# Query and key projections cut into two halves of 64 tokens, each on one half of TensorE's columns

## The chip, the cores and the metric

The kernel runs on one core of one Trainium2 chip. The metric is the time of one execution on the device, in microseconds (us); lower is better.

## What is computed

Linear attention over 4 batches, 4 heads, 1088 tokens and 32 dimensions per head, then two feed-forward layers on the 4352 x 128 result. The part that matters here is the feature map: queries and keys are multiplied by two small matrices, and the outer product of the two results is the feature vector.

```python
def phi(x):
    a = np.einsum('rd,bhsd->bhsr', S1, x)      # r = 8, d = 32
    b = np.einsum('rd,bhsd->bhsr', S2, x)
    return np.einsum('bhsi,bhsj->bhsij', a, b).reshape(*x.shape[:-1], r * r)
q_p, k_p = (phi(q), phi(k))
kv = np.einsum('bhsf,bhsd->bhfd', k_p, v)
z = np.sum(k_p, axis=2)
num = np.einsum('bhsf,bhfd->bhsd', q_p, kv)
den = np.einsum('bhsf,bhf->bhs', q_p, z)[..., None] + 1e-06
```

Behind it follow a gated feed-forward layer (rms norm, `silu(x @ w_gate) * (x @ w_val) @ w_out`, 1536 hidden) and a mixture layer with 32 slots. All of them are float32.

## The kernel before

The tokens are worked in nine tiles T of 512 (the last has 256). For every tile the feed-forward layer runs over f, twelve blocks of 128 hidden units: `ff_in` (mm3 at L635 to L637, called three matmuls a product, because each operand is split into a high and a low part), `ff_gate` (silu on ACT, product on DVE), `ff_high` and `ff_low` (the split of the hidden block) and `ff_out`. These 128x512 matmuls fill most of TensorE's time. In the first tile, `ff_out` takes whole float32 operands instead (L690).

Between them, attention for the next tile is worked in small steps. `k_chain(b)` prepares the keys of a batch: DVE transposes 32x32 blocks (L338), `Keys.project(g)` multiplies by `bdf`, a 128x64 matrix with S1 and S2 of four heads on its diagonal blocks, `halves` copies one half of the result (L279, ACT), `outer` forms the feature vectors (L284, DVE), and `sum` (L386) multiplies them with the values; the two heads of a pair go to partitions from 0 and from 64. `q_chain(T)` does the same for queries: `shuffle` (L495), `project` (L500), `halves`, `outer`, `back`, `attend` (L523; L530 for the last tile), division, rms norm, and a transposition (L584). `r_chain(T)` takes the layer's result to the mixture layer (L707, L710, L717).

In `project`, the tokens are the stationary operand (the weight load, 128 columns for 128 tokens) and `bdf` is the moving one (64 columns). Each projection writes 128 tokens x 64 values into a PSUM bank. A batch of keys has two groups (g = 0 and 1) of four such projections and a third group of 64 tokens left over (g = 2, through the transposition L341 of a 64-row tile); a tile of queries has four, the last tile two. A projection is one instruction of the program and, in float32, two passes in the trace, each a weight load (PEld) and a matmul (PE).

The first tile's attention and the first weights' conversion to float32 (`conv_w`, `f64_words`) are the front: its order is a table, `FRONT`, with filler matmuls (`keep_busy`, L298) between the steps, in which `kp:0`, `kp:1`, `qp` and `kp:2` are the projections. The front ends near 23.5 us. After it, a planner orders the instructions of each engine by its own model of their durations, within what data and the written order of some steps (`in_order`) allow. So a step's instructions can lie apart or between those of another step, and an edit to one step can move others.

Of the kernel before, what the change touches and what calls it, by code (L numbers as in the profile page):

```python
# [16 lines left out]
P = 128  # L17
# [31 lines left out]
def body(ctx, tc, q, k, v, s1, s2, wg, wv, wo, rg, phi, w1, w2, out):  # L49
    nc = tc.nc  # L50
    pe, act, dve, pool = nc.tensor, nc.scalar, nc.vector, nc.gpsimd
# [217 lines left out]
    bdf = bd.rearrange("p h r -> p (h r)")  # L269
# [39 lines left out]
    def bank():  # L309
        if not free:  # L310
            return aux()
        free.append(free.pop(0))
        tag = free[-1]
        return ps.tile([P, 512], F32, tag=tag, name=tag, bufs=3 if tag == "aux" else 2)

    class Keys:
# [34 lines left out]
        def project(self, g):  # L351
            n, pp = self.size(g)
            self.a[g] = bank()
            for t in range(n):
                o = self.a[g][:pp, 64 * t : 64 * t + 64]
                pe.matmul(o, self.kT[g][:, P * t : P * t + pp], bdf, start=True, stop=True)  # L356

        def halves(self, g, both=False):
            n, pp = self.size(g)
# [122 lines left out]
    class Queries:  # L482
# [14 lines left out]
        def project(self):  # L497
            self.a["q"] = bank()
            for h in range(self.n):
                pe.matmul(self.a["q"][:, 64 * h : 64 * h + 64], self.qD[:, P * h : P * h + P], bdf, start=True, stop=True)  # L500

        def halves(self):
            self.pq = work()[:, 0 : 256 * self.n].rearrange("p (f g n) -> p f g n", f=2, n=D)
# [664 lines left out]
    for T in range(NTILE):  # L1168
# [10 lines left out]
        o = [ps.tile([P, 512], F32, tag="gv"[(T + e) % 2], name="fo", bufs=2) for e in range(2 if T == 0 else 1)]  # L1179
# [54 lines left out]
```

## Time and profile before

| | us |
|---|---|
| median of 3 runs | 322.39 (322.32 to 322.49) |
| profiled execution | 322.96 |
| its span | 321.2 |
| PE busy | 308.1 |
| DVE busy | 235.7 |
| ACT busy | 185.8 |
| POOL busy | 61.8 |

The span runs from the first to the last instruction of the profiled execution; its own time holds some 1.8 us more around it. PE is TensorE's matmuls and PEld its weight loads, which overlap with PE. Matmuls are pipelined, so one row's duration is longer than the distance to the next row's start; how long a step takes is read from the starts.

### The profile page before, as it was taken

What the parts mean: (1) busy time and instruction counts of PE and PEld (TensorE: products, weight loads), DVE (VectorE), ACT (ScalarE), POOL (GpSimd) and SP (SyncE); (2) the same over time, 40 slices, a digit from 0 to 9 for tenths busy, and PEclk for the clock granted to TensorE, in tenths of its full rate; (3) what the DMA queues carried; (4) which work ended last, traced back from release to release, by engine and by line L of the source; (5) the groups of instructions that cost most, each with busy time, mean ns of one, the idle gap of its engine ahead of it and who ended that gap; (6) DMA issues with size and microseconds to landing.
All of it is one profiled execution on the core that took longest, in us unless ns stands there. A gap on an engine that the chain in (4) does not pass through costs nothing.

```text
span 321.2 us, 5509 instructions
## 1 busy us (share of the span) xinstructions
PE 308.1 (96%) x2011; PEld 244.7 (76%) x2011; DVE 235.7 (73%) x457; ACT 185.8 (58%) x417; POOL 61.8 (19%) x104
## 2 busy tenths in 40 slices
PE   8979989999999999999999999999999999999992
PEld 5756645788887878888888788888887878898482
DVE  4779966695888776966988858668778666664762
ACT  3767374456646457566563666565565665566451
POOL 3346499800021120001010100010020100003120
PEclk9999999999999999999999999999999999999998
DMA  7988000000007000000080000000890493000017
GB/s 200 300 292 207 5 0 1 2 0 2 0 3 204 1 2 0 2 0 0 4 202 1 3 0 2 0 0 14 299 230 2 138 300 87 0 2 0 2 40 241
DMA packets 31131, 22.40 MB, mean 70 GB/s; under 512 B 13056, under 2 KB 27136, under 8 KB 31104
## 3 DMA queue, kind: packets, MB, share of 16 engines
q1 hardware_dynamic: 30928, 21.98, 23.7%
q8 instruction: 16, 0.26, 0.4%
q10 hardware_dynamic: 176, 0.07, 0.2%
q14 instruction: 11, 0.09, 0.1%
HBM read 19.81 MB, written 2.23 MB: 69 GB/s over the span
## 4 chain that ended last, share of the span: by engine, by line
PE 82%; POOL 4%; DVE 4%; DMA 3%; SPq 2%; ACT 1%; issue 1%; DVEq 0%; POOLq 0%
PE v L635 7%; PE g L636 7%; PE g L635 7%; PE v L636 7%; PE v L637 7%; PE g L637 7%; PE o L637 7%; PE o L635 7%; PE o L636 6%; PE aux L523 3%; PE aux L386 2%; SPq L77 2%; DMA g_sb<-in_moe_rms_g_dram 2%; PE aux L356 2%; PE o L690 2%; PE aux L500 2%
## 5 line engine op out<-in xcount | busy, mean ns | idle before, releaser
L665 ACT ACTIVATE silu<-g 128x512 f32<-128x512 f32 (+1 forms) x103 | 60.3, 592 | 36.1 <-PE g L637 32.9
L675 ACT CAST hh<-hf 128x512 fp32r<-128x512 f32 x89 | 54.9, 617 | 39.3 <-DVE hf L666 37.9
L666 DVE TENSOR_TENSOR hf<-v,silu 128x512 f32<-128x512 f32 (+1 forms) x91 | 61.3, 679 | 20.3 <-PE v L637 12.4
L680 DVE TENSOR_TENSOR hl<-hf,hh 128x512 fp32r<-128x512 f32 x89 | 60.8, 687 | 17.6 <-ACT hh L675 15.9
L635 PE MATMUL g<-xh,wgh 128*128 128x512 f32 (+1 forms) x108 | 42.7, 398 | 2.1 <-ACT xh L591 0.9
L635 PE MATMUL v<-xh,wgh 128*128 128x512 f32 (+1 forms) x108 | 42.7, 396 | 0.6 <-DVE hh L666 0.6
L636 PE MATMUL g<-xh,wgl 128*128 128x512 f32 (+1 forms) x108 | 41.5, 384 | 0.8 <-POOL wgl L245 0.8
L636 PE MATMUL v<-xh,wgl 128*128 128x512 f32 (+1 forms) x108 | 42.0, 389 | 0.0
L637 PE MATMUL v<-xl,wgh 128*128 128x512 f32 (+1 forms) x108 | 41.0, 380 | 0.0
L637 PE MATMUL g<-xl,wgh 128*128 128x512 f32 (+1 forms) x108 | 41.0, 379 | 0.0
L635 PE MATMUL o<-hh,woh 128*128 128x512 f32 (+1 forms) x94 | 36.8, 392 | 0.0
L637 PE MATMUL o<-hl,woh 128*128 128x512 f32 (+1 forms) x94 | 36.6, 389 | 0.0
L636 PE MATMUL o<-hh,wol 128*128 128x512 f32 (+1 forms) x94 | 35.6, 379 | 0.0
L571 POOL TENSOR_SCALAR rs<-ss 128x4 f32<-128x4 f32 (+1 forms) x8 | 2.9, 356 | 130.2 <-ACT sq L564 130.2
L635 PEld LDWEIGHTS g<-xh,wgh 128*128 128x128 f32 x108 | 20.2, 188 | 9.5 <-ACT wgh L238 2.4
L636 PEld LDWEIGHTS g<-xh,wgl 128*128 128x128 f32 x108 | 20.4, 188 | 5.2 <-POOL wgl L245 1.7
L635 PEld LDWEIGHTS v<-xh,wgh 128*128 128x128 f32 x108 | 20.3, 188 | 5.2 <-DVE hh L666 1.0
L637 PEld LDWEIGHTS v<-xl,wgh 128*128 128x128 f32 x108 | 20.3, 188 | 4.3 <-issue 0.5
L636 PEld LDWEIGHTS v<-xh,wgl 128*128 128x128 f32 x108 | 20.4, 188 | 4.1 <-issue 0.5
L637 PEld LDWEIGHTS g<-xl,wgh 128*128 128x128 f32 x108 | 20.3, 188 | 3.7
L284 DVE TENSOR_TENSOR work<-asb,aux 128x512 f32<-128x512 f32 (+2 forms) x25 | 19.4, 804 | 2.4 <-ACT asb L279 2.3
L637 PEld LDWEIGHTS o<-hl,woh 128*128 128x128 f32 x94 | 17.7, 188 | 3.2 <-issue 0.2
(255 smaller groups left out, 515.1 us busy)
## 6 DMA issues: line engine op xcount, KB each, us to landing
ring<-in_moe_w_dram SPq DMA_DIRECT2D x12, 256.0 KB, 7.4
ring<-in_moe_w_dram SPq DMA_DIRECT2D x5, 512.0 KB, 5.8
ring<-in_k_dram SPq DMA_DIRECT2D x8, 256.0 KB, 3.1
qt<-in_q_dram SPq DMA_DIRECT2D x4, 512.0 KB, 5.4
ring<-in_v_dram SPq DMA_DIRECT2D x16, 128.0 KB, 4.6
ring<-in_moe_w_gate_dram SPq DMA_DIRECT2D x6, 256.0 KB, 8.2
ring<-in_moe_w_val_dram SPq DMA_DIRECT2D x6, 256.0 KB, 6.8
ring<-in_moe_w_out_dram SPq DMA_DIRECT2D x3, 512.0 KB, 4.9
```

The lines of the kernel that those rows point to most:

```text
L77: i = (on or nc.sync).dma_start(out=out, in_=in_)
L284: on.tensor_tensor(out=dst.rearrange("p g (r s) -> p g r s", s=R), in0=x1.unsqueeze(3).to_broadcast([pp, n, r, R]), in1=x2.unsqueeze(2).to ...
L356: pe.matmul(o, self.kT[g][:, P * t : P * t + pp], bdf, start=True, stop=True)
L386: pe.matmul(self.a["kv", hp][64 * h2 : 64 * h2 + D1, 64 * hp : 64 * hp + 64], va[:, h, 2 * i + g, :] if t < 8 else vr[:, h, :], self.pk[hp ...
L523: pe.matmul(o, pD[:, f, h, :], rhs, start=(f == 0), stop=(f == 1))
L635: first = pe.matmul(o, ah, bh, start=start, stop=False)
L636: pe.matmul(o, al, bh, start=False, stop=False)
L637: last = pe.matmul(o, ah, bl, start=False, stop=stop)
L665: mark["silu"] = act.activation(s[:, cs], g[:, cs], AF.Silu).ins
L666: mark["gate"] = mark["gate", T, f] = dve.tensor_tensor(out=hf32[T, f][:, cs], in0=v[:, cs], in1=s[:, cs], op=ALU.mult).ins
L675: act.copy(hh[T, f], hf32[T, f])
L680: dve.tensor_tensor(out=hl[T, f], in0=hf32.pop((T, f)), in1=hh[T, f].bitcast(F32), op=ALU.subtract)
```

## The change

Each projection of 128 tokens becomes two of 64 tokens. The first writes partitions 0 to 63 of the bank, the second partitions 64 to 127, so the two use different halves of TensorE's columns. The moving operand stays `bdf`, 64 columns, so each half streams as many columns as the whole did; its weight load has 64 columns instead of 128. The projections of 64 left-over tokens stay as they are. All 128 rows of the array are used, as before. 66 projections become 132; nothing else is edited.

```diff
--- before.py
+++ after.py
@@ -352,8 +352,10 @@
             n, pp = self.size(g)
             self.a[g] = bank()
             for t in range(n):
-                o = self.a[g][:pp, 64 * t : 64 * t + 64]
-                pe.matmul(o, self.kT[g][:, P * t : P * t + pp], bdf, start=True, stop=True)
+
+                for p in range(0, pp, 64):
+                    o = self.a[g][p : p + 64, 64 * t : 64 * t + 64]
+                    pe.matmul(o, self.kT[g][:, P * t + p : P * t + p + 64], bdf, start=True, stop=True)
 
         def halves(self, g, both=False):
             n, pp = self.size(g)
@@ -497,7 +499,9 @@
         def project(self):
             self.a["q"] = bank()
             for h in range(self.n):
-                pe.matmul(self.a["q"][:, 64 * h : 64 * h + 64], self.qD[:, P * h : P * h + P], bdf, start=True, stop=True)
+                for p in range(0, P, 64):
+                    o = self.a["q"][p : p + 64, 64 * h : 64 * h + 64]
+                    pe.matmul(o, self.qD[:, P * h + p : P * h + p + 64], bdf, start=True, stop=True)
 
         def halves(self):
             self.pq = work()[:, 0 : 256 * self.n].rearrange("p (f g n) -> p f g n", f=2, n=D)
```

Where lines of the change are named, `Keys.project` is at L358 and `Queries.project` at L504; lines behind are moved by 2 or 4 (mm3 is at L639 to L641, the sums of L386 at L388).

The planner's order moves with it. Three places, all on PE:

The queries of tile 3, behind the transposition L584 of tile 2's attention (T is the transposed queries, bd the matrix of S1 and S2, aux a PSUM bank). Before:

```order
L635 MATMUL o<-hh,woh 128x512
L636 MATMUL o<-hh,wol 128x512
L637 MATMUL o<-hl,woh 128x512
L584 MATMUL aux<-ident,x 128x128 x4
L500 MATMUL aux<-bd,T 128x64 x4
L635 MATMUL o<-hh,woh 128x512
L636 MATMUL o<-hh,wol 128x512
L637 MATMUL o<-hl,woh 128x512
L635 MATMUL o<-hh,woh 128x512
```

And with the change:

```order
L639 MATMUL o<-hh,woh 128x512
L640 MATMUL o<-hh,wol 128x512
L588 MATMUL aux<-ident,x 128x128 x4
L504 MATMUL aux<-bd,T 64x64 x5
L641 MATMUL o<-hl,woh 128x512
L504 MATMUL aux<-bd,T 64x64 x3
L639 MATMUL o<-hh,woh 128x512
L640 MATMUL o<-hh,wol 128x512
L641 MATMUL o<-hl,woh 128x512
```

Four projections in one run became eight halves in two runs, of five and three, with one feed-forward matmul between them.

The queries of tile 4. Before:

```order
L635 MATMUL o<-hh,woh 128x512
L636 MATMUL o<-hh,wol 128x512
L500 MATMUL aux<-bd,T 128x64
L637 MATMUL o<-hl,woh 128x512
L500 MATMUL aux<-bd,T 128x64 x3
L635 MATMUL o<-hh,woh 128x512
L636 MATMUL o<-hh,wol 128x512
L637 MATMUL o<-hl,woh 128x512
```

With the change:

```order
L639 MATMUL o<-hh,woh 128x512
L640 MATMUL o<-hh,wol 128x512
L504 MATMUL aux<-bd,T 64x64
L641 MATMUL o<-hl,woh 128x512
L504 MATMUL aux<-bd,T 64x64 x4
L639 MATMUL o<-hh,woh 128x512
L640 MATMUL o<-hh,wol 128x512
L504 MATMUL aux<-bd,T 64x64 x3
L641 MATMUL o<-hl,woh 128x512
L639 MATMUL g<-xh,wgh 128x512
```

Runs of one and three projections became runs of one, four and three halves.

The left-over keys of the last batch, ahead of the key sums (work holds the feature vectors, va the values). Before:

```order
L636 MATMUL g<-xh,wgl 128x512
L637 MATMUL g<-xl,wgh 128x512
L356 MATMUL aux<-bd,T 64x64
L635 MATMUL v<-xh,wgh 128x512
L636 MATMUL v<-xh,wgl 128x512
L637 MATMUL v<-xl,wgh 128x512
L386 MATMUL aux<-work,va 33x64 x16
L635 MATMUL o<-hh,woh 128x512
```

With the change:

```order
L640 MATMUL g<-xh,wgl 128x512
L641 MATMUL g<-xl,wgh 128x512
L358 MATMUL aux<-bd,T 64x64
L388 MATMUL aux<-work,va 33x64 x16
L639 MATMUL v<-xh,wgh 128x512
L640 MATMUL v<-xh,wgl 128x512
L641 MATMUL v<-xl,wgh 128x512
```

The 64-token projection, which stood alone between feed-forward matmuls, now stands directly ahead of the sums.

## Rows read from the trace of the kernel before

**Rows 1.** Stretches: busy us (instructions) of PE, PEld, DVE, ACT, POOL; clock, DMA, GB/s.
```profile
28.00:56.00 28.00, 25.36 (x101) 15.62 (x99) 22.56 (x40) 15.18 (x33) 22.09 (x31) 1.00 0.16 37
56.00:292.00 236.00, 235.71 (x1452) 194.59 (x1451) 178.52 (x326) 140.44 (x304) 22.00 (x41) 1.00 0.19 51
```

**Rows 2.** Timeline of PE, a run of four: start us, us, instructions.
```profile
67.96 0.39 PE L635 MATMUL o<-hh,woh 128*128 128x512 f32 x1
68.19 0.39 PE L636 MATMUL o<-hh,wol 128*128 128x512 f32 x1
68.42 1.00 PE L500 MATMUL aux<-bd,T 128*128 128x64 f32 x8
...
69.54 0.39 PE L635 MATMUL g<-xh,wgh 128*128 128x512 f32 x1
```

**Rows 3.** Timeline of PE, a run of two projections.
```profile
164.02 0.39 PE L637 MATMUL v<-xl,wgh 128*128 128x512 f32 x1
164.24 0.55 PE L356 MATMUL aux<-bd,T 128*128 128x64 f32 x4
...
164.92 0.39 PE L636 MATMUL g<-xh,wgl 128*128 128x512 f32 x1
```

**Rows 4.** Timeline of PE, a 64-token projection and the key sums.
```profile
115.66 0.39 PE L637 MATMUL g<-xl,wgh 128*128 128x512 f32 x1
115.97 0.33 PE L356 MATMUL aux<-bd,T 128*64 128x64 f32 x2
116.23 0.50 PE L635 MATMUL v<-xh,wgh 128*128 128x512 f32 x1
116.57 0.39 PE L636 MATMUL v<-xh,wgl 128*128 128x512 f32 x1
116.80 0.40 PE L637 MATMUL v<-xl,wgh 128*128 128x512 f32 x1
117.13 1.09 PE L386 MATMUL aux<-work,va 128*33 128x64 f32 x32
...
118.48 0.40 PE L636 MATMUL o<-hh,wol 128*128 128x512 f32 x1
```

**Rows 5.** Timeline of PE around L530; then what runs between 246.1 and 246.2 us.
```profile
245.86 0.39 PE L637 MATMUL o<-hl,woh 128*128 128x512 f32 x1
246.18 1.17 PE L530 MATMUL aux<-kvr,work 128*64 128x132 f32 x16
...
247.62 0.40 PE L636 MATMUL v<-xh,wgl 128*128 128x512 f32 x1
...
246.18 0.34 PE L530 MATMUL aux<-kvr,work 128*64 128x132 f32 x2
```

**Rows 6.** Weight loads of L356: timeline; then count, ns min/median/max, shapes.
```profile
9.55 0.19 PEld L356 LDWEIGHTS g<-bd,T 128*64 128x64 f32 x2
...
L356 PEld LDWEIGHTS g<-bd,T x10: 133/192/192, 7.3 to 9.6; 128*128 128x128 f32 x8, 128*64 128x64 f32 x2
```

**Rows 7.** Timeline of PE around the transposition L341.
```profile
56.18 0.27 PE L341 MATMUL aux<-ident,kr 64*128 64x64 f32 x1
56.38 0.66 PE L356 MATMUL aux<-bd,T 128*128 128x64 f32 x4
```

**Rows 8.** Timeline of PE around a run of two and a 64-token projection.
```profile
62.81 0.59 PE L690 MATMUL o<-hh,ring 128*128 128x512 f32 x1
63.23 0.81 PE L356 MATMUL aux<-bd,T 128*128 128x64 f32 x6
...
64.31 0.40 PE L636 MATMUL g<-xh,wgl 128*128 128x512 f32 x1
```

**Rows 9.** Timeline of ACT in the front, with its wait.
```profile
18.10 0.67 ACT L188 ACTIVATE cvt<-ring 128x512 f32<-128x512 f32 x1 [1.96 <-DMA ring<-in_moe_w_val_dram]
...
19.23 0.29 ACT L564 ACTIVATE sq<-x 128x128 f32<-128x128 f32 x1
```

**Rows 10.** Timeline of PE, its one wait between 56 and 292 us.
```profile
97.60 0.50 PE L635 MATMUL g<-xh,wgh 128*128 128x512 f32 x1 [0.27 <-ACT silu L665]
```

## The prediction

> **What bounds the kernel now.** I read the page first: of the engines PE is busy longest, 308.1 of 321.2 us. Then the stretches [rows 1]: from 56 to 292 us, at the full granted clock (1.00), PE is busy 235.71 of 236.00 us, while DVE and ACT have 57 and 96 us to spare. There every added 0.1 us of PE time is 0.1 us of the result. From 28 to 56 PE idles 2.6 us, waiting for the conversion of weights; before 28 us it runs filler matmuls. So I price the change on PE, stretch by stretch, from rows of single runs of matmuls. PE works in steps: a 128x512 feed-forward matmul starts every 0.23 us [rows 2], the yardstick below.
>
> **What a projection costs now.** The trace shows each projection as two passes (x8 for four), each with its own weight load. The run of four begins at 68.42; from the step before it (68.19) to the second step after it (69.54) are 1.35 us, less two steps of 0.23 is 0.89, or 0.223 us a projection [rows 2]. The run of two, 164.02 to 164.92, gives 0.44, again 0.22 [rows 3]. A run thus has no fixed price: the loads follow each other 0.11 us apart under the streams, and the neighbours are of the same full shape.
>
> **What a half projection will cost.** Runs on half the columns exist already. The 64-token projection of keys (128x64 weights, 64 streamed columns: exactly the new instruction) stands alone at 115.97. From 115.66 to 116.57 are 0.91 us, less 0.46: 0.45 us for only two passes [rows 4]. The sums of L386, which alternate between the two column halves with 33-wide weights and 64 streamed columns, take 1.68 - 0.46 = 1.22 us (116.80 to 118.48) for 32 passes [rows 4]. Counting two passes on opposite halves as one round, 0.45 = F + 2r and 1.22 = F + 16r: a round costs r = 0.055 us, and entering and leaving the half shape costs a fixed F = 0.34 us a run. The rows show where F lies: 0.31 us instead of 0.23 before the run (115.66 to 115.97), a first load that nothing hides, and a step of 0.34 after it (116.23 to 116.57).
>
> The round of the new shape, 64-wide weights with 64 streamed columns on both halves, isn't in the trace. Below it is the sums' 0.055. Above it is L530: 64-wide weights and 132 streamed columns on both halves, 245.86 to 247.62, so 1.30 us for 8 rounds; less F that is 0.12 a round [rows 5]. Its two halves do start together: two matmuls run in the first 0.02 us [rows 5]. I take 0.057, by the sums, because the stream is the same as theirs and two 64-wide loads are not further apart than that even on one half (0.19 us for two of at least 133 ns, so at most 0.057, [rows 6]). For F the same rows give 0.32 (sums, with rounds of 0.056) to 0.40 (L530, with rounds of 0.113); I take 0.35, one hundredth over the solved value for the second half that starts behind the first.
>
> So a run of n projections cost 0.223n and will cost 0.35 + 0.057 x 2n: 0.58 against 0.45 for two, 0.81 against 0.89 for four, 1.26 against 1.78 for eight. **Three projections is the break-even**, and the order of the program decides which lengths there are.
>
> **The sum after the front.** In the order of before, 54 projections stand in 21 runs there, most of two or four. 54 x 0.223 = 12.0 us go. In the new order the planner cuts the halves into 25 runs, some of odd length: 8, 4, 4, 5, 4, 8, 5, 3, 4, 4, 8, 1, 4, 3, 3, 3, 2, 4, 4, 8, 4, 4, 5, 3, 4 halves. An odd run pays a full round for its last half, so the rounds sum to 118 instead of 108.
> - rounds: 118 x 0.057 = 6.7 us
> - fixed price: 25 x 0.35 = 8.8 us
> - two pairs of runs lie around the 64-row transposition L341, which already breaks the sequence (0.20 us from it to the next run, [rows 7]). At the first, one F falls away but a second unhidden load stays: -0.30. At the second, attention (L523) stands on the other side, so only one run touches it, and I take a third of that: -0.10
> - of the three 64-token projections after the front, one stood behind a run of two and cost 1.50 - 0.42 - 0.23 - 0.45 = 0.40 us more (62.81 to 64.31, with 0.42 for the step of L690, [rows 8]); it now lies in the run of five and is in the rounds: -0.40. Another moves directly ahead of the L386 sums and shares their F: 0.45 - 0.11 = -0.34. The third stays alone: 0.
>
> 6.7 + 8.8 - 0.4 - 0.74 - 12.0 = +2.4 us. The run of eight near 28.6 us, which would be 0.08 cheaper, lies where PE waits anyway, which leaves 2.4 as it is to the digit given.
>
> **The front.** There the runs are long (sixteen halves of keys, eight of queries with the 64 left-over keys), and the halves do save PE time: a projection takes two rounds, 0.11 us, instead of 0.22, so twelve save up to 1.3 us, and the key sums could start that much sooner. I cost this at nothing. The cover is the load of the first weights: ACT waits 1.96 us for it until 18.10, and the squares of the first query tile stand behind that conversion in ACT's order, at 19.23 [rows 9]. The change moves neither ACT's nor DVE's order in the front, nor any DMA. If the cover were gone, up to 1.3 us would come off.
>
> **Other engines.** POOL's and SP's orders stay the same. ACT and DVE get the same instructions, in places in another order. Each halves copy (L279) waits for the last pass of its projections, which comes some 0.2 us sooner in a run of four and about when it did in a run of two; from 56 us on PE waits for another engine only once, for ACT (0.27 us, [rows 10]), and added PE time widens that slack.
>
> **Result.** The profiled execution took 322.96 us (span 321.2), 0.57 over the median of the runs. Its own time would become 325.4; against the median of 322.39 I forecast **324.8 us**. With F from 0.32 to 0.40 the sum goes from +1.6 to +3.6.
>
> **Rivals.**
> - *Shape changes cost less than in the rows.* If 25 runs paid no F, the streams alone would count: 6.7 instead of 12.0, about 317 us. The sign turns where F falls below 0.35 - 2.4/25 = 0.25 us. For it: the rounds do overlap two halves. Against it: three kinds of runs on column halves give 0.32, 0.34 and 0.40. The Trainium skill, "TensorEngine Tiling (Array Packing)", section Theoretical Speedup, promises up to 2x where the small dimension is at most 64; by that alone the 12.0 us would halve, to about 316 us. The trace bears this out for the rounds, 0.055 for two passes instead of 0.11 each, but not for a run of two or four with its F. Chance 0.07.
> - *Loads don't hide under streams.* Then a round costs a 64-wide load and a stream one after the other, 0.057 [rows 6] and 0.055 [rows 4], 0.11 us, and 118 rounds add 118 x 0.053 = 6.3 us: about 331 us. The Trainium skill, "TensorE: Matmul & The Clock Gate", Part 3, says that a weight load overlaps running matmuls only where the row groups differ; both halves here use all rows, so by that rule this would come. The trace disagrees: the sums use all rows too (128*33 in [rows 4]) and their rounds take 0.055. Chance 0.08.
> - *The front counts after all*: 1.3 us off, 323.5 us. Against it: the wait for the load. Chance 0.09.
> - *The pieces that could give way give way together.* The old order's wait at 97.60 (0.27 us, [rows 10]) falls away in the new one, F is 0.32 (0.75 less) and the front gives its 1.3: 2.4 - 2.3 = +0.1, so about 322.5 and no difference. New waits can come in the new order just as well. Chance 0.08.
>
> **How the numbers follow.** The forecast has 0.68. About 0.2% (0.64 us) is what a measurement can tell from no change. Faster: the first rival, 0.07. Same: the last, 0.08. Slower: the forecast, the loads and the front, 0.85. The range leaves out the first two rivals and keeps the others: 322.5 (the last rival's time) to 327.2 (the 326.0 of F = 0.40 and rounds of up to 0.067).
>
> **What would show it.** In the profile after: a run of eight halves spans about 0.5 us from first to last pass, the step into a run from a 512-column matmul is 0.31 to 0.32 us, the first step behind it 0.34; the projections' groups shrink in busy time while the feed-forward groups' mean durations grow a little; PE stays full from 56 to 292 us and that stretch grows by 2 to 3 us; the squares near 19.2 us don't move. I am wrong if a run of four halves costs under 0.4 us (fixed price too high), if eight halves span 0.9 us (loads not hidden), or if the change of time lies outside 56 to 292 us.

## The result: 3.4 us slower

The changed kernel takes 325.72 us (median of 4 runs, 325.33 to 326.15), the kernel before beside it 322.36 (321.97 to 322.49): 1.0103 times as long, 95% interval 1.0086 to 1.012. Timed again with the last experiments it took 325.29 against 322.39, 1.0096 (1.0074 to 1.0118). So the loss is 2.9 to 3.4 us, where +2.4 was forecast: right in sign, inside the range, and 0.5 to 1.0 us too small.

The profiled execution took 326.15 us, its span is 324.3. The engines' busy times on its page (us, share of the span, instructions):

```profile
PE 310.6 (96%) x2143; PEld 240.4 (74%) x2143; DVE 235.5 (73%) x457; ACT 186.2 (57%) x417; POOL 60.3 (19%) x104
```

PE is 2.5 us busier than before (308.1), with 132 matmuls more, though its weight loads fell from 244.7 to 240.4 us. DVE, ACT and POOL have not moved by more than 1.5 us. PE was the bound and became a longer one. The stretch that answers to [rows 1] shows it full, as the prediction had it:

```profile
56.00:292.00 236.00, 235.35 (x1523) 187.91 (x1520) 176.60 (x320) 137.57 (x299) 19.96 (x39) 1.00 0.19 51
```

The rows that answer to those of before, from PE's timeline (start us, us, what, count). First a run of eight halves, a tile of queries, where [rows 2] had four whole projections:

```profile
67.52 0.39 PE L640 MATMUL o<-hh,wol 128*128 128x512 f32 x1
67.84 0.69 PE L504 MATMUL aux<-bd,T 128*64 128x64 f32 x16
68.45 0.50 PE L641 MATMUL o<-hl,woh 128*128 128x512 f32 x1
68.79 0.39 PE L639 MATMUL g<-xh,wgh 128*128 128x512 f32 x1
```

The step into the run is 0.32 us, the one behind its first neighbour 0.34, where 0.23 is usual; all sixteen passes lie within the 0.61 us from 67.84 to 68.45. Together 68.79 - 67.52 - 0.46 = 0.81 us, against 0.89 whole. Then four halves of keys, where [rows 3] had a run of two:

```profile
165.49 0.39 PE L641 MATMUL v<-xl,wgh 128*128 128x512 f32 x1
165.80 0.45 PE L358 MATMUL aux<-bd,T 128*64 128x64 f32 x8
166.19 0.50 PE L639 MATMUL g<-xh,wgh 128*128 128x512 f32 x1
166.52 0.39 PE L640 MATMUL g<-xh,wgl 128*128 128x512 f32 x1
```

That is 1.03 - 0.46 = 0.57 us against 0.44. From 0.57 = F + 4r and 0.81 = F + 8r follow r = 0.06 and F = 0.33; the prediction had 0.057 and 0.35. And here is another tile of queries, which the planner cut into one, four and three halves:

```profile
127.22 0.39 PE L640 MATMUL o<-hh,wol 128*128 128x512 f32 x1
127.53 0.33 PE L504 MATMUL aux<-bd,T 128*64 128x64 f32 x2
127.79 0.50 PE L641 MATMUL o<-hl,woh 128*128 128x512 f32 x1
128.22 0.45 PE L504 MATMUL aux<-bd,T 128*64 128x64 f32 x8
128.61 0.50 PE L639 MATMUL o<-hh,woh 128*128 128x512 f32 x1
128.94 0.40 PE L640 MATMUL o<-hh,wol 128*128 128x512 f32 x1
129.27 0.45 PE L504 MATMUL aux<-bd,T 128*64 128x64 f32 x6
129.65 0.50 PE L641 MATMUL o<-hl,woh 128*128 128x512 f32 x1
129.98 0.39 PE L639 MATMUL g<-xh,wgh 128*128 128x512 f32 x1
```

Five feed-forward steps of 0.23 lie in these 2.76 us, which leaves 1.61 for the sixteen passes: twice the 0.81 of the same work in one run. What the prediction did not have is L534, the last tile's attention, which is no part of the edit. [Rows 5] had its sixteen passes in one run of 1.30 us; now they are twelve and four:

```profile
250.43 0.39 PE L641 MATMUL v<-xl,wgh 128*128 128x512 f32 x1
250.75 1.11 PE L534 MATMUL aux<-kvr,work 128*64 128x132 f32 x12
...
252.13 0.40 PE L639 MATMUL o<-hh,woh 128*128 128x512 f32 x1
...
255.10 0.39 PE L641 MATMUL g<-xl,wgh 128*128 128x512 f32 x1
255.42 0.67 PE L534 MATMUL aux<-kvr,work 128*64 128x132 f32 x4
...
256.35 0.40 PE L640 MATMUL v<-xh,wgl 128*128 128x512 f32 x1
```

1.70 - 0.46 = 1.24 and 1.25 - 0.46 = 0.79, 2.03 us in all: 0.73 us more. Only a part of this is a second fixed price. In the trace of the change the four passes at 255.42 start 0.11 to 0.16 us apart and so do the last four of the twelve: the cut left eight passes with no partner on the other column half. In the one run of before a pass starts every 0.056 us on average from the second round on. Eight times 0.056 is 0.45 us, an estimate from these starts; the other 0.28 is near F.

### The profile page after: what moved, and what is told of

Its sections match the earlier page's. It is cut to its first block, busy times and chain, and to the rows that moved or that the text cites. A ratio compares the mean times of both kernels' runs of the same rounds, so it can differ in the third digit from the quotient of the medians.

```text
span 324.3 us, 5777 instructions
## 1 busy us (share of the span) xinstructions
PE 310.6 (96%) x2143; PEld 240.4 (74%) x2143; DVE 235.5 (73%) x457; ACT 186.2 (57%) x417; POOL 60.3 (19%) x104
## 4 chain that ended last, share of the span: by engine, by line
PE 82%; DMA 5%; DVE 4%; SPq 3%; POOL 2%; issue 1%; ACT 1%; DVEq 0%; POOLq 0%
PE g L639 7%; PE v L639 7%; PE g L640 7%; PE v L640 7%; PE g L641 7%; PE v L641 7%; PE o L641 7%; PE o L639 6%; PE o L640 6%; DMA ring<-in_moe_w_gate_dram 4%; PE aux L527 4%; SPq L77 3%; PE aux L388 2%; PE o L694 2%; PE aux L504 2%; DMA kr<-in_k_dram 2%
## 5 line engine op out<-in xcount | busy, mean ns | idle before, releaser
L639 PE MATMUL g<-xh,wgh 128*128 128x512 f32 (+1 forms) x108 | 43.3, 403 | 2.7 <-ACT wgh L238 1.2
L639 PE MATMUL v<-xh,wgh 128*128 128x512 f32 (+1 forms) x108 | 43.2, 400 | 0.0
L641 PE MATMUL g<-xl,wgh 128*128 128x512 f32 (+1 forms) x108 | 41.5, 384 | 0.0
L641 PE MATMUL v<-xl,wgh 128*128 128x512 f32 (+1 forms) x108 | 41.3, 382 | 0.0
L641 PE MATMUL o<-hl,woh 128*128 128x512 f32 (+1 forms) x94 | 36.9, 393 | 0.0
L639 PE MATMUL o<-hh,woh 128*128 128x512 f32 (+1 forms) x94 | 36.8, 392 | 0.0
L639 PEld LDWEIGHTS g<-xh,wgh 128*128 128x128 f32 x108 | 20.4, 189 | 9.8 <-ACT wgh L238 2.5
L639 PEld LDWEIGHTS v<-xh,wgh 128*128 128x128 f32 x108 | 20.6, 191 | 4.5 <-issue 0.7
L641 PEld LDWEIGHTS v<-xl,wgh 128*128 128x128 f32 x108 | 20.5, 189 | 4.2 <-issue 0.2
L641 PEld LDWEIGHTS g<-xl,wgh 128*128 128x128 f32 x108 | 20.5, 189 | 4.1 <-issue 0.2
L641 PEld LDWEIGHTS o<-hl,woh 128*128 128x128 f32 x94 | 17.6, 188 | 3.9 <-issue 0.4
```

What stands on the lines that cost most here:

```text
L639: first = pe.matmul(o, ah, bh, start=start, stop=False)
L641: last = pe.matmul(o, ah, bl, start=False, stop=stop)
```

## The measure used below

Times of single runs scatter by 0.5 us or more, and the kernel before was timed anew beside each set of experiments (322.57, 322.12 and 322.39 us), so times of different sets are compared by their ratios to it. The experiments are also compared on one stretch of their profiles: from the start of the first feed-forward matmul to that of the last group (L690 of the kernel before). For the kernel before, profiled once more, and the change, profiled once more (timelines of PE; the second number is the row's length):

```profile
22.40 0.50 PE L635 MATMUL g<-xh,wgh 128*128 128x512 f32 x1 [0.93 <-ACT xh L591]
...
290.95 1.03 PE L690 MATMUL o<-hf,work 128*128 128x256 f32 x4
```

```profile
22.30 0.50 PE L639 MATMUL g<-xh,wgh 128*128 128x512 f32 x1 [0.93 <-ACT xh L595]
...
294.12 1.03 PE L694 MATMUL o<-hf,work 128*128 128x256 f32 x4
```

268.55 and 271.82 us, so +3.27. The first profile of before has 268.41 there: the stretch repeats to 0.14 us, though the two executions differ by 1.16 us ahead of it. The table has every run; "fixed" is what F = 0.35 a run and 0.057 a round give for that kernel's own list of runs; a cut of L534 is in it with the measured 0.73.

| kernel | stretch, us over before | fixed | time, us | ratio to before (95%) |
|---|---|---|---|---|
| the change, first profile | +3.73 | +3.1 | 325.72 | 1.0103 (1.0086 to 1.012) |
| change_again | +3.27 | +3.1 | 325.29 | 1.0096 (1.0074 to 1.0118) |
| front_only | +0.08 | 0.0 | 321.56 | 0.9965 (0.9951 to 0.9979) |
| mid_only | +3.24 | +3.1 | 325.20 | 1.0085 (1.0067 to 1.0102) |
| whole_together | -0.58 | 0.0 | 321.84 | 0.9972 (0.996 to 0.9985) |
| halves_together | -1.38 | -0.6 | 321.28 | 0.9957 (0.9943 to 0.9972) |
| before_again | 0 | 0 | 321.8 | one run |
| l534_whole | +2.65 | +2.35 | 324.72 | 1.0078 (1.0059 to 1.0098) |
| keys_only | +0.36 | +0.2 | 321.63 | 0.9983 (0.9971 to 0.9995) |
| queries_only | +2.99 | +3.2 | 324.11 | 1.006 (1.004 to 1.0079) |
| before_longer | 0.00 | 0.0 | 321.57 | 0.9973 (0.9962 to 0.9984) |
| halves_in_long_runs | +1.46 | -1.75 | 323.47 | 1.0035 (1.0024 to 1.0045) |
| long_runs_longer | +1.27 | -1.75 | 322.44 | 1.0008 (0.9993 to 1.0024) |

## The experiments

The theory is that each run of halves between full-width matmuls has a fixed price, so that the number of runs decides. Its rivals: halves are dearer each, wherever they stand; or the new order brings waits.

**Where the loss is: the front or behind it.** front_only takes the halves for the first batch's keys and the first tile's queries alone:

```diff
+            w = 64 if self.b == 0 else pp
...
+                for p in range(0, pp, w):
+                    o = self.a[g][p : p + w, 64 * t : 64 * t + 64]
+                    pe.matmul(o, self.kT[g][:, P * t + p : P * t + p + w], bdf, start=True, stop=True)
```

and likewise `w = 64 if self.T == 0 else P` for queries.

> Halves only in the first batch's keys and the first tile's queries; every other projection whole, and the order after the front as before. Prediction on record (front hidden by the weights' load): 322.4, no difference. Theory 'runs' as the profile after suggests (long runs save PE time; at the 60 us mark the changed kernel was 0.65 us ahead): about 321.7, ratio 0.998, and the feed-forward steps after 62 us 0.5 to 0.7 us earlier than before all the way to the end. Rival 'halves' (each half costs more wherever it stands, 0.037 us apiece): about 323.2.

mid_only has `self.b > 0` and `self.T > 0` in these places.

> Halves everywhere but in the front; order after the front as in the changed kernel. Theory 'runs': all of the loss and none of the front's gain, 322.4 + 3.4 + 0.65 = 326.4, ratio 1.0125. If the front had hidden nothing and given nothing: 325.7, as the changed kernel.

The whole loss is behind the front: mid_only has +3.24 us of the change's 3.27 in the stretch, front_only +0.08, and both begin it where before_again does (22.50, 22.40 and 22.40 us; single executions differ there, see below). Why does the front give nothing, when its projections do get shorter? DVE's timeline of before_again:

```profile
9.94 0.41 DVE L284 TENSOR_TENSOR pkr<-asb,g 64x256 f32<-64x256 f32 x1 [1.08 <-ACT asb L279]
...
11.48 0.51 DVE L193 TENSOR_SCALAR cvt<-cvt 128x512 f32<-128x512 f32 x1
```

and of front_only:

```profile
9.31 0.41 DVE L284 TENSOR_TENSOR pkr<-asb,g 64x256 f32<-64x256 f32 x1 [0.20 <-ACT asb L279]
...
11.49 0.43 DVE L193 TENSOR_SCALAR cvt<-cvt 128x512 f32<-128x512 f32 x1 [0.57 <-ACT cvt L188]
```

The feature vectors of the left-over keys, and those behind them, come 0.63 us sooner, and DVE then waits 0.57 us for the first weights' conversion, which starts the next step at the same time as before. The front's saving is real and is lost to that wait. front_only's time is 1.0 us under before all the same; some 0.7 of that lies behind the last matmul and goes without halves too, as before_longer shows below, and the other 0.3 is within the interval. mid_only has the same 0.7 in its favour, so its time shows 2.6 us of loss where its stretch shows 3.24.

**The same instructions in fewer runs.** `tc.high_priority()` around the two project loops, and around L534, makes the planner put most of them out in one piece. whole_together is the kernel before with it:

```diff
+            with tc.high_priority():
+                for t in range(n):
+                    o = self.a[g][:pp, 64 * t : 64 * t + 64]
+                    pe.matmul(o, self.kT[g][:, P * t : P * t + pp], bdf, start=True, stop=True)
```

> Whole projections as before, but those of one step get priority in the planner, which puts most of them into one run (four instead of one and three, or two and two). Theory 'runs': whole projections have no fixed price, so joining them gains nothing: 322.4 within 0.3. Rival 'order' (the new order's waits cost, not the shape): a shift of 1 us or more either way from reordering alone.

halves_together is the change with the same lines.

> The change, with the same priority: 17 runs of halves after the front instead of 25, mostly of eight, and L534 in one run again. Theory 'runs': 81 fewer... by the sum, 0.35 a run and 0.057 a round: -0.6 against before after the front and -0.65 in it, so 321.1, ratio 0.996, 4.5 us under the changed kernel. Rival 'halves': as many halves, so as slow as the changed kernel, 325.7. Rival 'order': moves as whole_together does, from 325.7.

This is the sharpest test: halves_together has as many halves as the change, 2143 matmuls, and takes 321.28 us: by the ratios some 4.5 us less, in the stretch 4.65. It is faster than before. Halves are thus not dearer each. Between the two versions kept together the halves gain 0.80 us in the stretch (formula 0.6), where with the planner's cuts they lose 3.3. A part of the better times belongs to the order: before_again has two waits of PE behind 56 us (grouped waits: us in total, times, longest), of which the first profile of before had only the first,

```profile
PE g L635 <- ACT silu L665: 0.3, 1, 0.3
PE aux L341 <- DMA kr<-in_k_dram: 0.2, 1, 0.2
```

and in both kernels kept together neither is left, which is up to 0.5 of whole_together's 0.58 us.

**The kernel before once more.** In all profiles taken since the first one of before, the stretch began 0.7 to 1.3 us earlier than there.

> The kernel before, profiled once more. In every profile taken since, the first feed-forward matmul starts some 1.0 us earlier than in the first profile of before (22.5 us from the span's start, against 23.56 there), also where the front of the program was left as it was. If that is a matter of the one execution, this profile shows it near 22.5 us and no wait of ACT near 2 us for the second value weights; if it belongs to the program (the order in which SP hands out the transfers), it shows 23.5 us and a wait near 2 us again.

It is a matter of the execution. ACT's timeline in before_again, for [rows 9]:

```profile
15.84 0.68 ACT L188 ACTIVATE cvt<-ring 128x512 f32<-128x512 f32 x1
...
18.07 0.31 ACT L564 ACTIVATE sq<-x 128x128 f32<-128x128 f32 x1 [0.98 <-DVE x L541]
```

The value weights, for whose load ACT waited until 18.10 in [rows 9], are there at 15.84, and the squares wait for DVE instead, 1.16 us earlier than there.

**L534 alone.** The change, with the priority around L534 and nothing else:

```diff
-                for e in range(2):
+                with tc.high_priority():
+                    for e in range(2):
...
```

> The change, with the attention matmuls of the last tile (line 534 of the change) kept together as one run of 16 passes; everything else as in the change. Theory 'runs' (each run of halves between full-width matmuls has a fixed price): the run cut into 12 and 4 passes cost 2.03 us against 1.30, so this one is 0.7 us under the change, near 324.9. Theory 'halves' (each half dearer wherever it stands): no difference to the change, 325.6. Theory 'order' (waits from the new order): no difference beyond 0.3.

PE's timeline:

```profile
250.29 0.39 PE L641 MATMUL v<-xl,wgh 128*128 128x512 f32 x1
250.61 1.17 PE L534 MATMUL aux<-kvr,work 128*64 128x132 f32 x16
...
252.05 0.40 PE L639 MATMUL o<-hh,woh 128*128 128x512 f32 x1
```

1.76 - 0.46 = 1.30 us, as before. The stretch is 0.62 us shorter than change_again's, and by the ratios (1.0078 against 1.0096 and 1.0103) the time 0.6 to 0.8 us. The cut of L534 is about a fifth of the loss.

**Keys and queries apart.** keys_only leaves `Queries.project` as it was, queries_only `Keys.project`.

> Halves for the keys alone; the queries projected whole, as before. Behind the front these are 22 of the 54 projections. Theory 'runs': the keys stand in runs of four or eight halves, break-even or nearly so, +0.2 us behind the front, and with the earlier start that the other kernels show, near 321.8. Theory 'halves': 22 of 54 parts of the loss of 3.4 us behind the front, +1.4, near 323.0. Theory 'order': the reordering around the query runs is gone, so near 321.8 as well.

> Halves for the queries alone; the keys projected whole, as before. Theory 'runs': the planner cuts the queries into runs of two to five halves and the attention of the last tile into two, +3.1 us behind the front (of it 0.7 for the attention), near 324.8. Theory 'halves': 32 of 54 parts of 3.4 us, +2.0, near 323.6. Theory 'order': as 'runs', in waits ahead of the query runs instead of in the runs.

The stretches add up: +0.36 and +2.99 make 3.35, against 3.27 for both. Counted again, the keys have 24 of the 54 projections behind the front (the expectations say 22) and bring a tenth of the loss; the queries' 30 and L534, which is cut in queries_only too, bring the rest. Were halves dearer each, it would be 1.5 and 1.9. Nor is it waits: queries_only has none on PE behind 56 us, and change_again has the two of before_again, 0.3 and 0.2 us. The difference is the runs. In keys_only the keys stand in ten runs there, all of four halves or more; in queries_only the queries stand in fifteen, seven of them of three halves or fewer.

**The time behind the last matmul.** In the profiles of four kernels the span ends 4.8 us behind the last matmul, in those of before, the change, the two kept together and l534_whole 5.3 to 6.0 us.

```diff
-        for _ in range(n):
-            pe.matmul(idle[0][:, 0:256], hot[:, 0:P], hot, start=True, stop=True)
+        for _ in range(n):
+            w = 128 if len(idle) < 25 else 256
+            idle[len(idle)] = None
+            for c in range(0, 256, w):
+                pe.matmul(idle[0][:, c : c + w], hot[:, 0:P], hot[:, c : c + w], start=True, stop=True)
```

> The kernel before, with the first 24 of the idle matmuls at its start issued as two of 128 columns instead of one of 256: the same stream, but 24 more matmuls and loads in TensorE's program. In the profiles so far the time behind the last matmul comes in two sizes, 5.5 to 6.0 us (before, the change, whole_together, halves_together, l534_whole) and 4.8 us (front_only, mid_only, keys_only, queries_only); in the first five SP's third transfer of the output takes 1.5 to 2.0 us to issue instead of 0.33, and a 16 KB packet of the queue that brings TensorE's program lands just ahead of it. Theory 'fetch': that packet comes some 60 TensorE instructions ahead of the end, its place goes by the program's length modulo 256, and 48 more instructions move it out of the way: 0.7 us under the kernel before, near 321.6, with 4.8 us behind the last matmul. Rival: the two sizes have another cause (the halves in the front, the planner's order): no difference to before.

321.57 us, 0.8 under before, with the same filler stream cut into 24 matmuls more. SP's queue at the end in before_again (start us, us to issue):

```profile
311.04 0.36 SPq L1196 DMA_DIRECT2D out_dram<-hf  x1
311.59 1.51 SPq L1196 DMA_DIRECT2D out_dram<-hh  x1
313.19 0.38 SPq L1196 DMA_DIRECT2D out_dram<-hl  x1
```

and in before_longer:

```profile
311.54 0.36 SPq L1199 DMA_DIRECT2D out_dram<-hf  x1
312.10 0.33 SPq L1199 DMA_DIRECT2D out_dram<-hh  x1
312.91 0.33 SPq L1199 DMA_DIRECT2D out_dram<-hl  x1
```

One issue is held for 1.2 us, and the end comes 5.5 us behind the last matmul instead of 4.8. Some 0.7 us of the times of front_only, mid_only, keys_only and queries_only is this, more than the whole gain of keys_only (0.5). The hold goes by the program's length: it is there in all seven profiles with 2011 or 2143 matmuls, smaller (0.85 us, one issue later) with 2139, and absent with 2035 (twice), 2075, 2079, 2119 and 2163. The traces bear out what was put down ahead of the run: the packet of program moved out of the way. The view of the DMA queues counts packets by their start; q8, called instruction there, is the queue of the program. In before_again, from 310.5 to 313 us:

```profile
q8 instruction: 1, 0.02, 3.2%
```

and in before_longer from 305 to 309.9 us, with none from 310.5 to 313:

```profile
q8 instruction: 1, 0.02, 1.5%
```

In before_again this 16 KB packet runs from 311.43 to 312.72 us, within the held issue (311.59 to 313.10); in before_longer from 309.74 to 310.92, where the first output issue begins. So it is in all profiles: in the seven with the long hold such a packet is under way when the held issue starts, or starts within 0.1 us, and the issue ends 0.3 to 0.4 us after it landed; with 2139 matmuls it runs from 313.02 to 314.28, the issue at 313.10 still takes 0.33 us, and the next, from 313.92, is held until 314.77; in the six without the hold no such packet is under way during these issues. Why the packet holds an issue, and why not that one, stays open. The change has the hold as the kernel before has it, so its loss is not touched by this.

**As few and as long runs as possible.** halves_in_long_runs transposes both groups of keys first and projects them in one run of sixteen halves (in two of the three batches behind the front; the planner cut the other into four, four and eight); the last tile's two projections stay whole. The new lines stand in place of the loop over the two groups:

```diff
+        yield POST, 1
+        with tc.issue_after(mark["gate"]):
+            k.transpose(0)
+            k.transpose(1)
+        yield PE, 0
+        with tc.high_priority():
+            k.project(0)
+            k.project(1)
+        yield POST, 1
+        k.halves(0)
+        k.outer(0)
+        k.transpose(2)
+        yield POST, 0
+        k.halves(1)
+        k.outer(1)
+        k.copy(2)
+        yield PE, 0
...
+            w = 64 if self.T < 8 else P
```

> Halves in as few and as long runs as the program allows: the project loops are given to the planner in one piece (high priority), the two groups of keys are transposed first and projected in one run of 16 halves, the last tile's queries (two projections, under the break-even of three) stay whole, and the attention of the last tile stays one run. Theory 'runs': the formula with F = 0.35 us per run and 0.057 us per two halves gives 1.75 us less than before, near 320.5. Theory 'halves': as many halves as in the change, so near 325. Theory 'order': waits for the transposes that now stand ahead of both groups eat part of it, 320.5 to 322.5. Theory 'fetch': its program is as long as the change's within 8 instructions, so it keeps the 5.5 us or more behind the last matmul.

long_runs_longer is this with the filler matmuls cut as in before_longer.

> As halves_in_long_runs, with the idle matmuls at the start cut as in before_longer. Theories 'runs' and 'fetch' together: 1.75 + 0.7 us less than before, near 319.9. If 'fetch' is wrong: the same as halves_in_long_runs.

A miss: 323.47 us, some 2 over halves_together. Waits came in, some of them in the middle of the feed-forward work, as the theory 'order' feared, though for more than transposes. PE's timeline of halves_in_long_runs around a batch of keys, and later:

```profile
55.08 1.15 PE L357 MATMUL aux<-bd,T 128*64 128x64 f32 x32
...
56.74 0.33 PE L357 MATMUL aux<-bd,T 128*64 128x64 f32 x2 [0.30 <-ACT T L344]
57.48 1.09 PE L387 MATMUL aux<-work,va 128*33 128x64 f32 x32 [0.41 <-DVE work L284]
...
61.55 0.53 PE L387 MATMUL aux<-work,va 128*33 128x64 f32 x12
...
62.90 0.31 PE L387 MATMUL aux<-work,va 128*33 128x64 f32 x4
...
129.12 0.40 PE L646 MATMUL o<-hl,woh 128*128 128x512 f32 x1
129.72 0.50 PE L644 MATMUL g<-xh,wgh 128*128 128x512 f32 x1 [0.20 <-ACT xh L600]
```

The projections are as cheap as computed: 32 passes, sixteen halves, in 1.15 us. But the copies and outer products of two groups now fall on ACT and DVE in one burst. The key sums (L387) wait for it and come in five pieces instead of one, and some feed-forward steps stand up to 0.76 us apart instead of 0.23 (0.60 in the rows) because their operands are converted late. By PE's starts the five pieces cost 4.3 us, where before_again's one run of sums costs 2.4, and four late steps behind 129 us 1.4 more: together about the 3.2 us by which the stretch missed the formula. The long runs were paid for elsewhere. long_runs_longer is 1.0 us faster; in the two profiles 0.2 of it lies in the stretch and 0.4 behind the last matmul, where the hold is gone. halves_together with a program length without the hold was not tried.

**The change again.**

> The change itself, beside the others on this chip: near 325.6, 3.2 to 3.4 us over before. If the half clock at 22 to 26 us in its first profile was a matter of that execution, this profile shows full clock there and the feed-forward matmuls behind it some 0.3 us earlier; if it belongs to the change, it shows it again.

The half clock was that execution's. Stretches of the change's first profile, then of change_again (busy us of PE, PEld, DVE, ACT and POOL, granted clock, DMA share, GB/s):

```profile
22.00:26.00 4.00, 3.49 (x9) 2.71 (x10) 3.07 (x5) 3.02 (x7) 1.95 (x3) 0.58 0.34 83
```

```profile
22.00:26.00 4.00, 3.60 (x14) 2.44 (x14) 3.44 (x6) 3.68 (x8) 2.16 (x4) 1.00 0.52 163
```

Nine matmuls instead of fourteen run there; the two levels of the clock are 1.2 and 2.4 GHz. By PE's starts the first eight feed-forward steps took 3.46 us instead of 1.95, but the two stretches end with 0.46 us of difference: change_again then waits 0.7 us for DVE's gate product (hh), which the slower execution does not, and the rest is not taken apart.

## Why the prediction was right, and its sum too small

- **The bound.** Right: the loss is PE time behind the front, in both profiles of the change and in mid_only.
- **What whole projections cost, and the round r.** Right. Runs of eight and four halves took 0.81 and 0.57 us as computed (0.81 and 0.58). The two halves' streams and loads overlap: sixteen passes in 0.61 us. With this the rival "loads don't hide" falls; its rule, of the Trainium skill, "TensorE: Matmul & The Clock Gate", Part 3, is not borne out by these rows, whose halves use all rows of the array.
- **The fixed price F.** Right: 0.33 by the rows of the change. With F the formula gives -0.6 for the halves kept together and +3.2 for queries_only, where -0.8 (beside whole_together) and +2.99 were measured; were halves dearer each, it would be +3.3 and +1.9. The rival "shape changes cost less" falls. Its rule, of the Trainium skill, "TensorEngine Tiling (Array Packing)", Theoretical Speedup, says up to 2x; the longest run behind the front in these kernels, sixteen halves, comes to 0.35 + 16 x 0.057 = 1.26 by the formula against 1.78 whole, 1.4x, and a run of four halves to 0.57 against 0.44, which is a loss.
- **The sum.** The step that failed is the list of what is re-cut. It followed the 25 runs of projections, and the three 64-token ones, but not the other column-half work in the planner's order, of which L534 lost its one run and, for half of its passes, the partner on the other column half: +0.73 us by the rows, 0.62 by l534_whole. 2.4 + 0.73 = 3.1, and the stretch has 3.27. The row of L530 stood in the prediction as a bound for r, and was not looked for in the new order.
- **The front.** The value, nothing, was right, but by luck: the cover was named wrongly. It is not the load of [rows 9], which was late in that one execution only, and the squares did move (18.07 in before_again, 18.18 in the change's first profile). It is a conversion of weights on ACT, for which DVE waits.
- **Other engines.** The slack of the one wait, 0.27 us at 97.60 [rows 10], was to widen so that the wait fell away; that did not come, in both profiles of the change PE still waits 0.3 us there.
- **The size.** 3.27 us in the stretch became 2.9 to 3.4 us in the medians; the ends of the executions, 0.2 us apart, account for part of that spread.

## What to carry to other kernels

Two halves on opposite columns do run side by side, but each run of them between full-width matmuls costs a fixed 0.33 to 0.35 us here, so count runs, and passes left without a partner, not instructions: a split pays from four whole projections upwards and loses below three. Ask the scheduler's order for the lengths of the runs, of all work in that shape and not only of what was edited, and keep a run together before splitting it: the priority alone turned a loss of 1% into a gain of 0.4%. Longer runs are not free either, since they hand their readers a burst.

## What the runs showed of the hardware that was not expected

- The issue of one output transfer was held by 1.0 to 1.7 us beyond its usual 0.33 in seven profiles, each time with a 16 KB packet of the program queue under way; in before_longer, with 24 matmuls more in the program, the packet came 1.7 us earlier and no issue was held. Some 0.7 us of the time hang on it. A kernel with a few instructions more can be faster for no reason of its own work.
- The same load of the same program was waited for until 18.10 us in one execution and was there by 15.84 in another; the first feed-forward matmuls stand 1.16 us apart.
- The same program had a granted clock of 0.58 from 22 to 26 us in one execution and 1.00 in another. PE had sat idle 0.93 us in both just ahead of the first feed-forward matmul. It came once more in halves_in_long_runs, from 44 to 47.5 us, at 0.54, where long_runs_longer had 1.00.
